# The first MLP's first tiles in four parts, pooled maxima scaled on ScalarE, and a new order of issue

## The chip, the cores and the metric

The kernel runs on one core of a Trainium2 chip. A core has five engines with an instruction stream each: TensorE (PE in the profile; its weight loads are listed as PEld), VectorE (DVE), ScalarE (ACT), GpSimd (POOL) and SyncE (SP), which here only issues DMAs. The engines wait for each other through semaphores, and each works through its own stream in the order in which the program was written. The metric is the device time of one launch in microseconds; the median of three runs is compared.

## What is computed

Two attentions over the same q, k and v are added, one over positions pooled in fours and one over a band of seven neighbours; the sum is the input of two MLPs in a row.

```python
q_d = q.reshape(B, H, Sd, 4, D).mean(axis=3)          # B=4, H=8, S=576, Sd=144, D=64
out_d = sm_attn(q_d, k_d, v_d)                        # softmax attention, pooled
out_up = np.repeat(out_d, 4, axis=2)
mask = np.abs(pos[:, None] - pos[None, :]) < 4        # the band
out_local = softmax(where(mask, q @ k.T / 8, -1e9)) @ v
x = (out_up + out_local).transpose(0, 2, 1, 3).reshape(2304, 512)
h = x @ moe_w_in                                      # 512 -> 2048
x = np.maximum(0.01 * h, h) @ moe_w_out               # 2048 -> 512
h = x @ moe2_w_in
out = where(h >= 1, h, where(h <= -1, 0, (h + 1) ** 2 / 4)) @ moe2_w_out
```

## The kernel before

**Tiling.** The 2304 tokens go through each MLP in five blocks of 512, 512, 512, 512 and 256. Every MLP operand is held as two f16 halves, high and low, and a product is three products of halves (high by high, high by low, low by high). In the first MLP `g1` (L1922) makes one tile of the hidden layer, 128 features by 512 tokens: twelve 128x512 matmuls (L1934), three for each of the four 128-row chunks `c` of the input, into one PSUM bank. A chunk `c` of the input is one pair of heads. ACT and DVE turn the tile into two halves (L2046, L2172, L2176), and `g2` (L2196) adds its share of the second product into four further banks. The second MLP makes each product by a seven-product scheme on half-size operands: `s1` to `s4` (products at L1964) with copies on ACT (L1995) and sums on DVE (L2003, L2006, L2013) between them, and then two passes over the second weight (`pass1`, `pass2`, products at L2133), whose results are drawn together on DVE (`onto`, L2154) and stored (L2165).

**Attention.** `prep` (L1128) loads q and k and transposes them on PE (L1185), with copies on ACT (L1209). `local_p` does the banded attention of the first 16 of 36 pieces as matmuls (scores L1497 to L1512, row maximum on DVE at L1525, exponent on ACT at L1530, transposes L1553, product with v L1570, result to f16 halves at L1594 and L1600); `local_d` does the others on DVE alone (L1705 to L1779). `down` does the pooled attention, one pair of heads at a time: sums of four on DVE (L1278, L1280, L1287), scores on PE (L1353), then, for each of the two heads, `peak` on DVE (L1367 takes the maximum, L1368 multiplies it by minus the scale), `pexp` on ACT (L1375, two exponents that take the result as bias), the reciprocal, `norm` (on DVE at L1392, or on ACT at L1388 for the batches in `NORM_ACT_D`), transposes (L1402) and the product (L1420).

**Weights.** They come as 64-bit numbers and are turned into f16 halves: three DVE operations on integers (L701, L707, L713), one on ACT (L727) and one on DVE (L729) for the first MLP, and a like chain (L852 to L877) for the second, which then also needs sums of quarters (L961, L1056, L1063).

**What sets the order.** The program is written by a planner, `Issue.run`: all operations are given a key (a due time in steps of the MLPs, shifted by tables such as `DUE`, `G2LATE`, `LAG7`, `PASS2`), an estimated duration and their dependences, and the planner plays the five engines forward in time. Whenever an engine is free in its estimate, it takes the ready operation with the lowest key. What results is a fixed order for each engine. Where PE has nothing ready in the plan before the time `FILL`, the planner writes in a product with zeros (L2529, 128x512, called a filler below), which keeps PE's clock up and whose result nobody reads. After `FILL` an idle PE in the plan leaves no trace in the program.

**PSUM.** There are eight banks, handed out by `Banks`; once the MLPs have begun, six of the eight are kept for them.

Of the kernel before, what the change touches and what calls it, by code (L numbers as in the profile page):

```python
# [15 lines left out]
AX = mybir.AxisListType.X  # L16
# [11 lines left out]
LEAD_O = 2  # L28
WINDOW_O = 15
OUT_GAP = 0.411  # L30
LAG7 = {0: 10, 1: 9, 2: 15, 3: 18, 4: 10}
# [4 lines left out]
T4_LATE = 12  # L36
EARLY_O = 4
W1_SPARE = 1957
LATE1 = 5.273
# [4 lines left out]
WINDOW_T = 7  # L44
# [5 lines left out]
WINDOW_A = 19  # L50
WINDOW_D = 15
LEAD_W = 6
LEAD_W1 = 1.5
LEAD_W1O = 1.477
RUSH_B = {1: 7.782}
RUSH_P = None
W1_RUSH = 0
QUEUE = 2.793
# [3 lines left out]
WINDOW_B = {2: 6, 3: 6}  # L62
# [5 lines left out]
DMA_END = 1.377  # L68
SW_END = 2.263
# [6 lines left out]
RUN_PE = 0.06  # L76
# [6 lines left out]
D_PE = 24.191  # L83
D_STRETCH = 1.006
W1_FROM = 9
W1_MORE = 1.467
# [10 lines left out]
PEAK_D = 4921  # L97
RESERVE = 3947
HP_GAP = 0.8
RESERVE_W = 0  # L100
SPARE = 5950

TWO_FROM = (2, 98)
WINDOW = 22
WINDOW_W = 34
LIMIT = 26744
AHEAD = 5
LEAD_Q = (12, 8)
O_LATE = 1.34
LAGMAX = 5  # L110
G2KEY = 1.87

NORM_ACT = (1,)
NORM_ACT_D = (1,)
FILL = 173.83


DUE = {0: -0.12, 2: 0.03, 3: -0.01, 9: 2.8, 10: -0.4, 14: -3.31, 17: -9.75, 19: -0.21,
# [129 lines left out]
class Issue:  # L248
# [4 lines left out]
    SHAPE = 0.093  # L253

# [36 lines left out]
    def run(self, fill=None):  # L291
# [16 lines left out]
        while left:  # L308
# [94 lines left out]
class Banks:  # L403
# [24 lines left out]
def kernel(  # L428
# [36 lines left out]
    QB = 64  # L465
# [48 lines left out]
    T_SC = 0.553  # L514
# [222 lines left out]
    class Pair:  # L737


        def __init__(self, n, nu):  # L740
# [3 lines left out]
            self.ready = []  # L744

# [1823 lines left out]
```

## Time and profile before

| | us |
|---|---|
| median of 3 runs (820.48 to 821.06) | 820.82 |
| the profiled execution | 821.11 |
| its span, first to last instruction | 819.3 |
| PE busy | 812.0 |
| DVE busy | 726.5 |
| ACT busy | 499.1 |

The profiled execution has 1.8 us outside its span. A PE matmul is listed with its whole way through the array, 379 ns for 128x512, while the next one begins 216 ns after it: neighbouring matmuls overlap, and the pace is read from starts, not from durations. For the same reason the profile calls PE busy while a filler runs. An idle time is printed with the engine and line that ended it.

### The profile page before, as it was taken

The numbers are of one execution on the slowest core, as the hardware profiler recorded it, in microseconds if no ns is written. First come the engines' busy times: TensorE is split into PE (matmuls) and PEld (weight loads), VectorE is DVE, ScalarE is ACT, GpSimd is POOL, SyncE is SP. The second block draws the span as 40 slices with busy tenths as digits, with TensorE's granted clock in tenths as the row PEclk, the third lists the DMA queues.
The fourth block names the chain that finished last, engine by engine and source line by source line (L and its number), as shares of the span: only waits on it lengthen the run. The fifth ranks groups of instructions, "written<-read, shape, count | busy, mean of one in ns | idle before, by whom it ended". The sixth has DMA issues, their size and how long they took to land. (4 is left out here: it accounts for less than half of the span.)

```text
span 819.3 us, 17419 instructions
## 1 busy us (share of the span) xinstructions
PE 812.0 (99%) x6791; PEld 562.6 (69%) x6791; DVE 726.5 (89%) x1360; ACT 499.1 (61%) x1283; POOL 38.7 (5%) x60
## 2 busy tenths in 40 slices
PE   9999999999999999999999999999999999999997
PEld 6765554544454444544446888888888888889986
DVE  4999999999999999999999999999669697896761
ACT  4987667466436463473356677777567676775640
POOL 1010000033001310000000000000000000000000
PEclk9999999999999999999999999999999999999999
DMA  8877556576345822331733320010000200100001
GB/s 207 207 193 232 190 187 172 155 145 126 92 124 168 134 44 69 100 103 55 253 103 129 110 73 27 2 52 27 26 2 14 78 14 2 52 27 2 3 27 52
DMA packets 63521, 77.40 MB, mean 94 GB/s; under 512 B 17742, under 2 KB 41678, under 8 KB 63438
## 3 DMA queue, kind: packets, MB, share of 16 engines
q1 hardware_dynamic: 52238, 72.13, 28.4%
q0 software_dynamic: 11200, 4.15, 4.5%
q8 instruction: 53, 0.87, 0.4%
q14 instruction: 30, 0.25, 0.1%
HBM read 66.80 MB, written 9.44 MB: 93 GB/s over the span
## 5 line engine op out<-in xcount | busy, mean ns | idle before, releaser
L1934 PE MATMUL bank<-arena,w 128*128 128x512 f16 (+1 forms) x960 | 197.0, 358 | 0.0
L2196 PE MATMUL bank<-arena,w 128*128 128x512 f16 x768 | 176.4, 379 | 0.3 <-DVE arena L2176 0.3
L1934 PEld LDWEIGHTS <-w 128*128 128x128 f16 x960 | 92.5, 98 | 88.9 <-issue 1.9
L2196 PEld LDWEIGHTS <-w 128*128 128x128 f16 x960 | 92.0, 98 | 86.9 <-issue 2.3
L2133 PEld LDWEIGHTS <-w 128*128 128x128 f16 x1086 | 106.0, 98 | 12.2
L2133 PE MATMUL bank<-arena,w 128*128 128x256 f16 x810 | 96.8, 273 | 0.0
L1964 PEld LDWEIGHTS <-w 128*128 128x128 f16 x960 | 86.4, 98 | 10.0 <-issue 1.3
L2046 ACT ACTIVATE arena<-bank 128x512 f32<-128x512 f32 x64 | 38.0, 593 | 81.5 <-PE bank L1934 79.2
L2050 ACT ACTIVATE w<-bank,half 128x512 f32<-128x512 f32 x66 | 45.3, 687 | 41.5 <-DVE bank L2013 38.8
L1964 PEld LDWEIGHTS <-arena 128*128 128x128 f16 x720 | 64.8, 98 | 6.7
L2099 ACT ACTIVATE w<-w 128x256 f16<-128x256 f32 (+1 forms) x112 | 50.2, 478 | 17.4 <-DVE w L2058 13.2
L1964 PE MATMUL bank<-arena,w 128*128 128x256 f16 (+1 forms) x480 | 59.9, 267 | 0.6 <-DVE bank L2006 0.4
L2058 DVE SCALAR_TENSOR_TENSOR w<-w,bank 128x512 f32<-128x512 f32 x66 | 44.8, 681 | 15.0 <-ACT w L2054 14.0
L2103 DVE SCALAR_TENSOR_TENSOR w<-w 128x256 f16<-128x256 f32 (+1 forms) x112 | 53.1, 502 | 3.6 <-ACT w L2099 3.5
L1964 PE MATMUL bank<-w,w 128*128 128x256 f16 (+1 forms) x480 | 52.6, 256 | 0.0
L1995 ACT COPY w<-bank 128x256 f32<-128x256 f32 x106 | 36.4, 365 | 18.2 <-PE bank L1964 16.5
L2133 PEld LDWEIGHTS <-arena 128*128 128x128 f16 x426 | 41.6, 98 | 5.5 <-issue 0.7
L1964 PE MATMUL bank<-arena 128*128 128x256 f16 (+1 forms) x384 | 44.6, 266 | 0.0
L2176 DVE SCALAR_TENSOR_TENSOR arena<-arena 128x512 f16<-128x512 f32 x64 | 43.6, 682 | 0.3 <-ACT arena L2172 0.3
L1779 DVE TENSOR_TENSOR arena<-arena 128x768 f32<-128x768 f32 (+2 forms) x60 | 41.1, 687 | 1.4
L2054 ACT ACTIVATE w<-w 128x512 f32<-128x512 f32 x66 | 41.1, 628 | 1.2
L2172 ACT ACTIVATE arena<-arena 128x512 f16<-128x512 f32 x64 | 40.3, 630 | 0.9
(219 smaller groups left out, 1342.0 us busy)
## 6 DMA issues: line engine op xcount, KB each, us to landing
arena<-in_moe_w_in_dram SPq DMA_DIRECT2D x15, 1024.0 KB
arena<-in_moe_w_out_dram SPq DMA_DIRECT2D x8, 1024.0 KB
arena<-in_moe_w_out_dram SPq DMA_DIRECT2D x9, 512.0 KB
arena<-x SPq DMA_DIRECT2D x4, 1024.0 KB
x<-arena SPq DMA_DIRECT2D x15, 256.0 KB
w<-in_moe_w_out_dram SPq DMA_DIRECT2D x7, 512.0 KB
out_dram<-w SPq DMA_DIRECT2D x14, 256.0 KB
arena<-in_k_dram SPq DMA_DIRECT2D x23, 112.0 KB
```

The costliest lines, as they stand in the source:

```text
L1779: nc.vector.tensor_tensor(out, x, y, op=ALU.add)
L1934: nc.tensor.matmul(h[:, e], a[:, f // FP, c, f % FP], y[:, :, c, :], start=(n == 0), stop=(n == 3 * KDM - 1),)
L1964: nc.tensor.matmul(o[:, e], a[:, i, c], y[:, k, c, :], start=first and e == 0 and n == 0, stop=n == 5, skip_group_check=True,)
L2050: nc.scalar.activation(out=t, in_=st["h", p], func=AF.Relu, scale=0.5 * s_in, bias=half)
L2054: nc.scalar.activation(out=t, in_=t, func=AF.Square, scale=s_in ** -0.5)
L2058: nc.vector.scalar_tensor_tensor(out=t, in0=t, scalar=1.0 / s_in, in1=st["h", p], op0=ALU.min, op1=ALU.max)
L2099: nc.scalar.activation(out=left(p, part, q0, q1)[:, 0], in_=src(), func=AF.Copy, scale=so)
L2103: nc.vector.scalar_tensor_tensor(out=d[:, 1], in0=src(), scalar=so, in1=d[:, 0], op0=ALU.mult, op1=ALU.subtract)
L2133: nc.tensor.matmul(o[:, k], a[:, i, at:at + P], y[:, j], start=opens and p == e == k == n == 0, stop=p == PH - 1 and e == E - 1 and n == 2 ...
L2172: nc.scalar.activation(out=gv(p)[0], in_=st["t", p].ap, func=AF.Copy, scale=so)
L2176: nc.vector.scalar_tensor_tensor(out=lo, in0=st["t", p].ap, scalar=so, in1=hi, op0=ALU.mult, op1=ALU.subtract)
L2196: nc.tensor.matmul(o, a, y[:, e, :], start=(first and n == 0 and c % E == 0), stop=(last and n == 2), skip_group_check=True,)
```

## The change

The first three tiles (`EARLY = 3`) of the first MLP's first block are no longer made by one operation of twelve matmuls that waits for the whole input block. Each is four operations of three matmuls, one for each pair of heads, chained to one another, and each waits only for that pair's own part of the input (`x.by[c]`) and the weights. The bank is taken with the first part and stays taken until ACT has read the tile.

In `down` the maximum is taken with its sign turned (one DVE instruction), and the multiplication by the scale moves to ACT, as a small instruction ahead of the two exponents. `NORM_ACT_D` takes in batch 2, so the four normalisations of that batch (one DVE instruction on 72x576 each) become 16 on ACT (72x144 each).

The planner's estimates are altered: a result that is used on the engine that made it is ready at once, where 0.14 to 0.25 us were allowed before, and some durations and DMA latencies have other values. All tables of keys are new, so nearly every instruction stands elsewhere. A line of them and the rest of the diff:

```diff
-G2LATE = {0: 7.366, 1: 6.364, 2: 4.968, 3: 5.548, 4: 9.226}
-PASS2 = {0: 47.587, 1: 3.15, 2: 56.047, 3: 70.737, 4: 41.965}
+G2LATE = {0: 7.696146, 1: 10.971802, 2: 1.675998, 3: 4.854888, 4: 14.291468}
+PASS2 = {0: 45.397812, 1: 23.065416, 2: 37.189274, 3: 77.327851, 4: 66.686012}
+EARLY = 3
+EARLY_ROOM = 0
-NORM_ACT_D = (1,)
-FILL = 173.83
+NORM_ACT_D = (1, 2)
+FILL = 170.7754
...
-                    u.ready = max(u.ready, d + self.HOP[op.eng]
-                                  + (self.HOP_PE if u.eng == "PE" else 0.0))
+                    hop = 0.0 if u.eng == op.eng and not op.lat else (
+                        self.HOP[op.eng] + (self.HOP_PE if u.eng == "PE" else 0.0))
+                    u.ready = max(u.ready, d + hop)
...
+    def hold(self):
+        self.mlp += 1
+        return self.get()
...
-            nc.vector.reduce_max(ml(0, par), psv(par), axis=AX)
-            nc.vector.tensor_scalar_mul(ml(0, par), ml(0, par), -s_e)
+            nc.vector.reduce_max(ml(0, par), psv(par), axis=AX, negate=True)
 
         def pexp(par):
             if not par:
                 st["p"] = buf(4 * G, from_t)
             p = st["p"].ap[:GH].rearrange("p (h a g) -> p h a g", h=2, a=2)
+            nc.scalar.mul(ml(0, par), ml(0, par), s_e)
...
         x1[blk].ready.append(o)
+        x1[blk].by[hp].append(o)
...
-        def g1(p, i):
-            sch.step = max(sch.step, i)
-            h_open[0] += 1
+        def g1(p, i, cs=range(KDM)):
+            if KDM - 1 in cs:
+                sch.step = max(sch.step, i)
+                banks.begun = True
...
-            st["h", p] = banks.get(True)
+            if 0 in cs:
+                h_open[0] += 1
+                st["h", p] = banks.hold()
...
-                n = 0
-                for c in range(KDM):
+                n = 3 * cs[0]
+                for c in cs:
...
-            o1 = sch.add(
+            o1 = None
+            if m == 1 and not b and p < EARLY:
+                for c in range(KDM):
+                    o1 = sch.add(
+                        "PE", 3 * t_mm(N) * E, lambda p=p, i=i, c=c: g1(p, i, (c,)),
+                        x.by[c] + [o1] + [w_ready[m, 0, f] for f in fs], key=float(i),
+                        banks=0 if c else 1, mlp=True, cols=3 * 512,
+                        gate=None if c else (lambda: len(banks.free) > EARLY_ROOM))
+            o1 = o1 or sch.add(
```

How it moves the instructions, at three places. The first is PE's stream where the first MLP begins; L2529 and L2554 are the fillers, L1934 and L1951 the products of `g1`, in the kernel before and in the changed one. Before:

```order
L1185 MATMUL bank_64<-ident,arena 64x64 x8
L2529 LDWEIGHTS zeros
L2529 MATMUL bank_63<-zeros 128x512
...
L1353 MATMUL bank_67<-w_61 72x144
L1353 MATMUL bank_69<-w_61 72x144
...
L1934 LDWEIGHTS w_79
L1934 MATMUL bank_68<-arena,w_79 128x512
...
L1934 MATMUL bank_65<-arena,w_79 128x512
...
L2529 LDWEIGHTS zeros
L2529 MATMUL bank_70<-zeros 128x512
```

And after:

```order
L1523 MATMUL bank_66<-arena 64x70 x8
L1951 LDWEIGHTS w_79
L1951 MATMUL bank_69<-arena,w_79 128x512
...
L1581 MATMUL bank_65<-arena 64x64 x8
L1581 MATMUL bank_70<-w_61,arena 64x64 x8
...
L1564 MATMUL bank_70<-ident,w_61 70x128 x4
L1951 LDWEIGHTS w_79
L1951 MATMUL bank_69<-arena,w_79 128x512
...
L2554 LDWEIGHTS zeros
L2554 MATMUL bank_63<-zeros 128x512
```

Before, two whole tiles (banks 68 and 65) stand in a row once the attention of the block is through, after three fillers; after, the first tile (bank 69) stands in threes between the products of the last pairs of heads. The stream as a whole has 51 fillers before and 41 after, and the same number of each other product.

The second place is where the pooled maxima stand on DVE, first before and then after:

```order
L1367 TENSOR_REDUCE w_61<-bank_69 72x2
L1368 TENSOR_SCALAR w_61<-w_61 72x2
L1278 TENSOR_TENSOR arena<-arena 72x4x128
L1280 TENSOR_TENSOR w_61<-arena 72x2x2x64
L1367 TENSOR_REDUCE w_61<-bank_64 72x2
```

```order
L1378 TENSOR_REDUCE w_61<-bank_70 72x2
L1536 TENSOR_REDUCE w_61<-bank_65 128x4
L1378 TENSOR_REDUCE w_61<-bank_64 72x2
L1298 TENSOR_REDUCE w_61<-w_61 128x144
L1289 TENSOR_TENSOR arena<-arena 72x4x128
```

and on ACT after, where L1384 is the new multiplication and L1386 the exponents:

```order
L1384 ACTIVATE w_61<-w_61 72x2
L1386 ACTIVATE w_61<-bank_70,w_61 72x144 x2
L1220 ACTIVATE w_61<-bank_66 128x64x5
L1541 ACTIVATE w_61<-bank_65,w_61 128x70 x4
L1568 COPY w_61<-bank_67 70x512
L1220 ACTIVATE w_61<-bank_68 128x64x4
L1384 ACTIVATE w_61<-w_61 72x2
```

DVE has one instruction less for each of the 32 maxima, and ACT one more, which stands directly ahead of the exponents that need it; eight of the 32 stand in the attention of the first batch.

The third place is the end of PE's stream, where the last two blocks' second passes stand; the rows are those at which the bank changes. Before:

```order
L2133 MATMUL bank_64<-arena,w_79 128x256
...
L2133 MATMUL bank_63<-arena,w_79 128x256
...
L2133 MATMUL bank_67<-arena,w_79 128x256
...
L2133 MATMUL bank_64<-arena 128x256
...
L2133 MATMUL bank_70<-arena,w_79 128x256
```

And after:

```order
L2150 MATMUL bank_63<-w_79 128x256
...
L2150 MATMUL bank_69<-arena 128x256
...
L2150 MATMUL bank_64<-arena,w_79 128x256
...
L2150 MATMUL bank_63<-arena,w_79 128x256
...
L2150 MATMUL bank_64<-arena,w_79 128x256
```

Before, the last bank (70) belongs to a 512-token block, and DVE's last instruction reads 128x512 of it for a store of 256 KB. After, the long stretch of the 512-token block (bank 69) stands further forward, between the passes of the 256-token block, whose last read is 128x256 for a store of 128 KB.

## Rows read from the trace of the kernel before

**Rows 1.** The page: span, busy time and instructions of each engine

```profile
span 819.3 us, 17419 instructions
...
PE 812.0 (99%) x6791; PEld 562.6 (69%) x6791; DVE 726.5 (89%) x1360; ACT 499.1 (61%) x1283; POOL 38.7 (5%) x60
```

**Rows 2.** Busy us by stretch (A:B length, PE, PEld, DVE, ACT, POOL, clock, DMA, GB/s)

```profile
0.00:40.00 40.00, 38.80 (x637) 27.11 (x639) 28.02 (x89) 28.05 (x125) 5.39 (x24) 1.00 0.80 208
40.00:80.00 40.00, 40.00 (x511) 24.99 (x506) 38.60 (x101) 32.34 (x117) 4.04 (x8) 1.00 0.76 211
...
520.00:560.00 40.00, 39.64 (x363) 35.24 (x361) 39.08 (x85) 30.23 (x64) 0.00 (x0) 1.00 0.10 34
560.00:600.00 40.00, 40.00 (x369) 35.86 (x367) 31.76 (x68) 24.61 (x54) 0.00 (x0) 1.00 0.06 21
```

**Rows 3.** What PE waited for: us in total, times, longest us

```profile
PE bank L2529 <- DVE half L533: 1.2, 1, 1.2
PE bank L2133 <- DVE w L2154: 0.5, 1, 0.5
PE bank L1964 <- DVE bank L2006: 0.4, 1, 0.4
PE bank L2196 <- DVE arena L2176: 0.3, 1, 0.3
PE bank L1964 <- DVE bank L2013: 0.2, 1, 0.2
```

**Rows 4.** PE's timeline near 115 us: start us, us, line, operation

```profile
113.56 1.04 PE L2529 MATMUL bank<-zeros 128*128 128x512 bf16 x4
114.52 0.57 PE L1570 MATMUL bank<-w,arena 70*64 70x64 f32 x12
...
115.25 2.75 PE L1934 MATMUL bank<-arena,w 128*128 128x512 f16 x12
```

**Rows 5.** DVE's timeline there: the low half of a weight

```profile
113.40 1.22 DVE L729 SCALAR_TENSOR_TENSOR w<-w,w 128x1024 f16<-128x1024 f32 x1
```

**Rows 6.** DVE's timeline near 18 us

```profile
17.85 0.45 DVE L1367 TENSOR_REDUCE w<-bank 72x2 f32<-72x288 f32 x1
18.33 0.17 DVE L1368 TENSOR_SCALAR w<-w 72x2 f32<-72x2 f32 x1
18.41 0.68 DVE L1278 TENSOR_TENSOR arena<-arena 72x512 f32<-72x512 f32 x1
...
20.58 0.45 DVE L1525 TENSOR_REDUCE w<-bank 128x4 f32<-128x280 f32 x1
20.95 0.74 DVE L1287 TENSOR_REDUCE w<-arena 128x144 f32<-128x576 f32 x1
```

**Rows 7.** By source line: duration ns min/median/max, first and last start

```profile
L1367 DVE TENSOR_REDUCE w<-bank x16: 443/446/454, 17.9 to 136.6; 72x2 f32<-72x288 f32 x16
...
L1392 DVE TENSOR_TENSOR arena<-arena x8: 746/748/748, 195.9 to 331.4; 72x576 f32<-72x576 f32 x8
```

**Rows 8.** ACT by line and shape, first 60 us: its smallest work

```profile
L1375 ACT ACTIVATION_READ_ACCUMULATOR w<-bank,w 72x1 f32 x6 | 1.2, 208 | 0.0
...
L1594 ACT ACTIVATE arena<-w 128x64 f16<-128x64 f32 x4 | 1.0, 258 | 0.0
```

**Rows 9.** The end: DVE's last reads

```profile
806.88 0.42 DVE L2154 SCALAR_TENSOR_TENSOR w<-bank,w 128x256 f32<-128x256 f32 x1 [3.58 <-PE bank L2133]
...
814.67 0.69 DVE L2154 SCALAR_TENSOR_TENSOR w<-bank,w 128x512 f32<-128x512 f32 x1 [4.55 <-PE bank L2133]
```

**Rows 10.** The end, busy us by stretch: a store of 128 KB, one of 256 KB

```profile
808.10:808.70 0.60, 0.60 (x8) 0.53 (x7) 0.00 (x0) 0.00 (x0) 0.00 (x0) 1.00 0.63 219
...
816.20:817.20 1.00, 0.00 (x0) 0.00 (x0) 0.00 (x0) 0.00 (x0) 0.00 (x0) 1.00 0.74 262
```

**Rows 11.** SP's timeline: the first load of q for batch 1

```profile
25.93 0.36 SPq L1140 DMA_DIRECT2D arena<-in_q_dram  x1
```

**Rows 12.** PE's timeline: the first use of it

```profile
38.13 1.26 PE L1185 MATMUL bank<-ident,arena 64*64 64x64 f32 x36
```

More of the change, by code (lines that the diff above doesn't have):

```diff
@@ L27 @@
 OUT7 = (0,1,2,3,4)
-LEAD_O = 2
+LEAD_O = 5
 WINDOW_O = 15
-OUT_GAP = 0.411
-LAG7 = {0: 10, 1: 9, 2: 15, 3: 18, 4: 10}
-G2LATE = {0: 7.366, 1: 6.364, 2: 4.968, 3: 5.548, 4: 9.226}
-PASS2 = {0: 47.587, 1: 3.15, 2: 56.047, 3: 70.737, 4: 41.965}
+OUT_GAP = 0.357325
+LAG7 = {0: 9, 1: 10, 2: 18, 3: 18, 4: 12}
+G2LATE = {0: 7.696146, 1: 10.971802, 2: 1.675998, 3: 4.854888, 4: 14.291468}
+PASS2 = {0: 45.397812, 1: 23.065416, 2: 37.189274, 3: 77.327851, 4: 66.686012}
 SOON = 1000.0
 FP = 2
-T4_LATE = 12
+EARLY = 3
+EARLY_ROOM = 0
+T4_LATE = 10.083883
 EARLY_O = 4
-W1_SPARE = 1957
-LATE1 = 5.273
+W1_SPARE = 4178
+LATE1 = 8.896926
 LEAD_S = 4
@@ L43 @@
 LEAD_T = 4
-WINDOW_T = 7
+WINDOW_T = 9
 LEAD = 5
@@ L49 @@
 RUSH = 1.0e4
-WINDOW_A = 19
-WINDOW_D = 15
+WINDOW_A = 17
+WINDOW_D = 13
 LEAD_W = 6
-LEAD_W1 = 1.5
-LEAD_W1O = 1.477
-RUSH_B = {1: 7.782}
+LEAD_W1 = 1.06903
+LEAD_W1O = 1.731533
+RUSH_B = {1: 6.558924}
 RUSH_P = None
 W1_RUSH = 0
-QUEUE = 2.793
+QUEUE = 2.681077
 WHOLE = ()
@@ L61 @@
 POOLED = ()
-WINDOW_B = {2: 6, 3: 6}
+WINDOW_B = {2: 8, 3: 6}
 LEAD_D = 2
@@ L67 @@
 DMA_LAST = 0.85
-DMA_END = 1.377
-SW_END = 2.263
+DMA_END = 1.710062
+SW_END = 1.886638
 SW_FIRST = 1.88
@@ L75 @@
 RUNS = (0, 1)
-RUN_PE = 0.06
+RUN_PE = 0.061
 RUN_ACT = 1.1
@@ L82 @@
 LAT_W = (1.95, 1.95)
[L83 to L86, printed above, removed]
+D_PE = 80
+D_STRETCH = 0.856281
+W1_FROM = 6
+W1_MORE = 1.972363
 D_ACT = (0,1)
@@ L96 @@
 ADD_PE = ()
-PEAK_D = 4921
-RESERVE = 3947
-HP_GAP = 0.8
+PEAK_D = 5103
+RESERVE = 218
+HP_GAP = 0.756178
 RESERVE_W = 0
-SPARE = 5950
+SPARE = 5409
 TWO_FROM = (2, 98)
-WINDOW = 22
-WINDOW_W = 34
-LIMIT = 26744
+WINDOW = 27
+WINDOW_W = 24
+LIMIT = 26572
 AHEAD = 5
-LEAD_Q = (12, 8)
-O_LATE = 1.34
+LEAD_Q = (10, 5)
+O_LATE = 4.600221
 LAGMAX = 5
-G2KEY = 1.87
+G2KEY = 0.5
 NORM_ACT = (1,)
-NORM_ACT_D = (1,)
-FILL = 173.83
-DUE = {0: -0.12, 2: 0.03, 3: -0.01, 9: 2.8, 10: -0.4, 14: -3.31, 17: -9.75, 19: -0.21,
[7 rows of a table removed]
+NORM_ACT_D = (1, 2)
+FILL = 170.7754
+DUE = {0: -0.01, 2: -0.09, 3: -10.68, 4: 1.18, 5: -0.17, 7: -0.38, 9: 8.62, 10: -0.31,
[9 rows of a table added]
 class Arena:
@@ L253 @@
     SHAPE = 0.093
+    SAME = True
     FREE = 0.14
@@ L744, in __init__ @@
             self.ready = []
+            self.by = {c: [] for c in range(KDM)}
         def make(self):
@@ L1225, in prep @@
                 n = (NA, QBB - NA)[i]
-                t = ch.op("PE", pe_mm(RUN_PE * 2 * n, QB, 2 * n, D) if b in RUNS else pe_tr(QB, n, QB), lambda nm=nm, i=i: tr(nm, i), [ld[nm]], banks=1, shape=(1, 1) if b in RUNS else (2, 2),
+                t = ch.op("PE", pe_mm(0.05 + RUN_PE * 2 * n, QB, 2 * n, D) if b in RUNS else pe_tr(QB, n, QB), lambda nm=nm, i=i: tr(nm, i), [ld[nm]], banks=1, shape=(1, 1) if b in RUNS else (2, 2),
                           after=(lambda nm=nm: st[nm].free(),) if i else ())
@@ L1447, in down @@
         for par in range(2):
-            e = ch.op("DVE", 0.56, lambda par=par: peak(par), [o, e], need=() if par else (8,))
-            x = ch.op("ACT", 2 * t_act(G, True, 2), lambda par=par: pexp(par), [e, x],
+            e = ch.op("DVE", t_dve(2 * G), lambda par=par: peak(par), [o, e], need=() if par else (8,))
+            x = ch.op("ACT", 2 * t_act(G, True, 2) + 0.1, lambda par=par: pexp(par), [e, x],
                       need=() if par else (4 * G,),
@@ L1861, in local_d @@
                 reds.append(o)
-            o = ch.op("DVE", 0.36 + 0.16 * sum((r == 0) + (r + n == SEGB) for _, n, _, r in rr),
+            o = ch.op("DVE", 0.36 + 0.32 * sum((r == 0) + (r + n == SEGB) for _, n, _, r in rr),
                       lambda par=par: soft1(par), reds, need=(L,))
@@ L1898, in local_d @@
                 ch.op("DVE", t_dve(512), lambda jh=jh: xl(jh), [h], after=freer(("x", jh))))
+            for by in x1[blk].by.values():
+                by.append(ch.ops[-1])
         ch.close()
```

2 lines of the change are left out of this document (1 added, 1 removed), and 16 rows, old and new, of the table DUE.

## The prediction

> **What bounds the kernel now.** I read the page first, then busy time by stretches of 40 us, then what PE waited for, then single places in the timelines. The page says that PE is busy for 812.0 of 819.3 us [rows 1]. That could mean that only PE's own work counts. But the stretches show that DVE is as full as PE for two thirds of the span: 38.6 of 40 us between 40 and 80 us, 39.1 between 520 and 560 us (the stretches between are like these two), and only from 560 us on does it fall to 31.8 [rows 2]. And each wait of PE that the profile prints, after the start, ended with a DVE instruction: 0.5, 0.4, 0.3 and 0.2 us, together 1.4 us [rows 3]. So PE and DVE run level up to about 560 us, and PE alone sets the pace behind that. The granted clock is 1.00 in every stretch, 2.4 GHz, and is not in play. The first 40 us are another regime: DVE and ACT are busy for 28 us each and wait for loads and for each other [rows 2], and PE fills its holes with products of zeros.
>
> Of those there are 51 before and 41 after. They are real time on PE, and the other products are the same in number, so the change can gain on PE in two ways only: fewer fillers and fewer waits.
>
> **The change part by part.**
>
> *Fillers.* Four in a row take from 113.56 to 114.52 us, 0.24 us each [rows 4]. Ten fewer: 10 x 0.24 = 2.4 us less on PE. At the pace of 216 ns of two 512-column products in a row it is 2.2 us; I take 2.4.
>
> *Whether DVE can follow.* The fillers at 113.56 cover a wait: the weight half that DVE makes from 113.40 to 114.62 us [rows 5] is of the kind that the product at 115.25 [rows 4] multiplies with, and between its end and the product lie 0.6 us. So of a group of fillers the last half microsecond or so is more than the wait needed, and the rest stood for DVE. If PE is to run 2.4 us earlier from here on, DVE must deliver some 1.8 us earlier. It gets this from two edits. A maximum with its scaling takes from 17.85 to 18.41 us, 0.56 us; a reduction of nearly the same size that is not followed by a user of its result takes from 20.58 to 20.95, 0.37 us [rows 6]. The sign in the instruction and the scaling on ACT thus save 0.19 us for each of 32 maxima. Sixteen of them stand before 137 us [rows 7], 16 x 0.19 = 3.0 us; the others are in the later batches, 3.0 us more. The four normalisations of batch 2 that leave DVE have 0.75 us each, about 0.67 in a stream where neighbours overlap, 2.7 us in all, after 190 us [rows 7]. So DVE has 3.0 us by 137 us, more than the 1.8 that it needs, and 8.7 us by 331 us. I charge nothing here; the price of a failure is the 2.4 us (first rival).
>
> *Waits of PE.* With DVE that far ahead, the 0.3 us at L2196, in the middle of the kernel, should go. The 0.5 us at L2133 is at the very end, where PE waits for DVE to have read the bank that it writes next; in the new order 48 products of another block stand between, so it goes. The 0.4 and 0.2 us at L1964 [rows 3] come from the chain copy, sum, product inside the second MLP, and I leave two thirds of them. Sum: -1.0 us, of at most -1.4 and at least 0.
>
> *The end.* DVE's last read becomes one of 256 columns instead of 512: 0.42 instead of 0.69 us [rows 9]. The last store becomes one of 128 KB: such a one moved within 0.6 us, one of 256 KB needed 1.0 us [rows 10]. Nothing else runs there, so both count in full: -0.27 - 0.4 = -0.7 us.
>
> *ScalarE.* It gets 32 small multiplications and 16 normalisations. No row shows a multiplication of 72x2. The nearest are the read of an accumulator, 0.21 us for one column, and a scaling of 64 columns, 0.26 us [rows 8]. After 40 us ACT has idle time to hide them, 7.7 us in the stretch from 40 to 80 [rows 2], and no wait of PE was ended by ACT [rows 3], so these 40 cost nothing; uncovered, the 24 multiplications among them alone would be 24 x 0.21 = 5.0 us. But eight multiplications stand in the attention of the first batch, at the start, where each of the three engines waits for the others. From below their cost is zero, since the chain of one pair of heads is no longer than before: 0.17 us of scaling on DVE [rows 6] goes, about 0.21 on ACT comes. From above it is 8 x 0.26 = 2.1 us, if ACT's stream is what the start waits for. ACT is busy for 28.0 of the first 40 us [rows 2], and part of the 12 idle ones lies before the first data; I take 0.8 us, a little under half of 8 x 0.21.
> The Trainium skill ("ScalarE: Activation LUTs", section "Rules for kernel authors") speaks against this edit: it tells one to put a multiplication on VectorE, not ScalarE. The same page (section "What ACT_TABLE_LOAD costs") gives 186 ns for an operation with constants as scale and bias, plus 0.83 ns an element, so an estimate by it is 0.19 us each, 1.5 us for the eight with nothing hidden. No run here shows the operation yet.
>
> *The product in four parts.* The products stay twelve to a tile, so PE's work is as before; the parts of the first tile fill holes between other products in the attention of the last pairs of heads. That is where fillers went, so the gain is in the first term. The wait that is new is that of a part for its pair of heads: PE works in order, and all of its stream is queued behind. The bank that the tile holds for longer is one of eight. I take zero.
>
> *The second MLP's order.* The number of products between a copy's source and the user of the sum falls from 18 to 12 at four places by the new order. The wait that such a place showed was 0.4 us [rows 3]; four of them would be 1.6, none 0. I take one, +0.4 us.
>
> **Sum:** -2.4 - 1.0 - 0.7 + 0.8 + 0.4 = -2.9 us. The profiled execution has 821.11 us, of which 819.3 are its span, so 818.2 for it. The median lies 0.29 below it at 820.82; from there, **817.9 us**.
>
> **The rivals.**
>
> *First, no change: the fillers come back as waits.* PE has 10 fillers fewer, but DVE, ACT and the loads deliver when they did, and what DVE saves is lost in waits of its own. For it: DVE and PE are level, so any hole of DVE is at once one of PE. Against it: the DVE work that goes is more than is needed. The 2.4 us return: 820.3 us.
>
> *Second, no change: ACT becomes the bound of the start.* The eight multiplications cost 2.1 us instead of 0.8, and the start moves by 1.3 us: 819.2 us. For it: the three engines wait for each other there; against it: ACT is 30% idle.
> This is what the rule of the Trainium skill ("ScalarE: Activation LUTs", "Rules for kernel authors") amounts to here.
>
> *Third, faster still.* All 1.4 us of waits go, ACT hides all and the second MLP's new order costs nothing: -2.4 - 1.4 - 0.7 = -4.5, 816.3 us.
>
> *Fourth, slower: loads at the start.* The new order of SP's DMAs puts weights further forward. Up to and with batch 1's first load of q, 6.70 MB are asked for instead of 5.65; at 208 GB/s [rows 2] the 1.05 MB are 5.0 us. Before, that load is issued at 25.93 us [rows 11] and its data are used at 38.13 [rows 12], 12.2 us later; 5.0 us later and used about 1.3 us earlier, by the products that stand ahead of it, 5.9 us are left. That is enough for 0.3 MB at this rate. If the queues are deeper than that, PE waits there with all of its stream behind it. A delay of 5 us more than that slack would give 817.9 + 5 = 822.9 us; it turns the sign from 2.9 us on. For it: the DMA engines are 80% busy at the start [rows 2]. Against it: SP itself waits for buffers more than the data wait for a queue.
>
> That the change does not do what it says is excluded by the order: 41 fillers, 36 instructions fewer on DVE and 48 more on ACT are there.
>
> **How the numbers follow.** A measurement of this kernel can tell about 0.2% (1.6 us) from no change, that is, times under 819.2 or over 822.5 us. My forecast has 0.47, the first rival 0.20, the second 0.10, the third 0.10, the fourth 0.13. Faster: 0.47 + 0.10 = 0.57; same: 0.20 + 0.10 = 0.30; slower 0.13. The range goes from the third case, 816.3, to 821.2: that takes in both cases of no change with some of the upper ends of the unknown costs (0.9 us above 820.3), and leaves out the fourth.
>
> **What would show it.** Right: PE's busy time down by about 2.4 us, with no new wait of PE over 0.5 us before 60 us; the instruction at the new maximum taking 0.37 us to the next; the wait at the last passes gone; DVE's last read 0.42 us long. The first rival would show as PE waits between 40 and 200 us that add up to about 2 us, ended by DVE or ACT. The second as an ACT that is busy 30 us or more of the first 40 and ends PE's waits. The fourth as a wait of PE at the transposes (L1185 before) ended by a DMA. The forecast is wrong if PE's waits as a whole exceed those of before.

## The result, and the profile after

The change makes the kernel slower. After: 825.79 us, median of 6 runs (823.96 to 828.19). Before, on the same chip: 820.69 us, median of 6 (820.45 to 822.38). The ratio is 1.0061 with a 95% interval of 1.0043 to 1.0078, so +5.1 us. The forecast was 817.9, 7.9 us too low, and the result lies outside its range of 816.3 to 821.2. The profiled execution of after has 825.57 us, of which 823.8 are its span.

The page of after, span and busy time, against [rows 1]:

```profile
span 823.8 us, 17396 instructions
...
PE 812.9 (99%) x6781; PEld 562.1 (68%) x6781; DVE 726.1 (88%) x1324; ACT 515.8 (63%) x1331; POOL 38.8 (5%) x60
```

DVE has 36 instructions fewer, and yet its busy time went down by 0.4 us only, from 726.5 to 726.1. Keep that row in mind: it holds most of the answer. PE's busy time, which was to fall by about 2.4 us, rose by 0.9.

Busy time by stretches of 40 us, the kernel after (columns as in [rows 2]):

```profile
0.00:40.00 40.00, 38.49 (x605) 26.77 (x607) 27.52 (x79) 26.96 (x118) 4.02 (x22) 1.00 0.98 227
40.00:80.00 40.00, 39.84 (x515) 24.61 (x512) 39.11 (x96) 31.01 (x106) 3.30 (x9) 1.00 0.74 197
...
360.00:400.00 40.00, 38.91 (x186) 18.06 (x184) 38.97 (x55) 19.86 (x51) 0.00 (x0) 1.00 0.29 96
...
440.00:480.00 40.00, 38.59 (x337) 32.80 (x336) 39.62 (x54) 24.94 (x41) 0.00 (x0) 1.00 0.46 159
480.00:520.00 40.00, 39.03 (x357) 34.67 (x356) 39.12 (x77) 32.26 (x65) 0.00 (x0) 1.00 0.04 15
520.00:560.00 40.00, 40.00 (x368) 35.72 (x366) 34.70 (x76) 30.27 (x65) 0.00 (x0) 1.00 0.10 34
```

The same stretches before, where they did not stand in [rows 2]:

```profile
360.00:400.00 40.00, 39.91 (x190) 18.46 (x188) 39.56 (x56) 15.46 (x26) 0.00 (x0) 1.00 0.35 122
...
440.00:480.00 40.00, 39.79 (x352) 34.26 (x351) 39.86 (x53) 25.98 (x44) 0.00 (x0) 1.00 0.37 133
480.00:520.00 40.00, 39.99 (x367) 35.67 (x366) 39.79 (x84) 33.44 (x70) 0.00 (x0) 1.00 0.04 15
```

The start is nearly as it was. The loss lies in the middle: in the nine stretches from 160 to 520 us PE is idle for 5.3 us, before for 0.6, and DVE is full there in both kernels. The clock is 1.00 in all of these stretches. Lined up in the two traces by the share of its columns that PE has done (fillers left out, f32 columns counted four times), PE is 1.4 us ahead of before at 32% (202 us) and 5.5 us behind at 68% (519 us). So a part of the gain was there at first and was lost later.

What PE waited for in the kernel after, against [rows 3]:

```profile
PE bank L2213 <- DVE arena L2193: 1.9, 4, 1.1
PE bank L2554 <- DVE half L543: 1.2, 1, 1.2
PE bank L1981 <- ACT w L2012: 1.1, 1, 1.1
PE bank L1981 <- DVE bank L2023: 1.0, 2, 0.7
PE bank L1951 <- ACT arena L1386: 0.5, 1, 0.5
PE bank L1981 <- DVE w L2075: 0.2, 1, 0.2
PE bank L1951 <- DVE arena L1755: 0.2, 1, 0.2
PE bank L1413 <- ACT w L1541: 0.2, 1, 0.2
```

Without the start (L2554) that is 5.1 us where the forecast had 0.4 of 1.4 left. None of these waits was ended by a load. DVE ends 3.3 us of them: it is late, although it was given less work. ScalarE ends 1.8 us, where before it ended none.

The end is what was forecast. DVE's last reads, against [rows 9]:

```profile
817.54 0.42 DVE L2171 SCALAR_TENSOR_TENSOR w<-bank,w 128x256 f32<-128x256 f32 x1 [4.55 <-PE bank L2150]
820.24 0.43 DVE L2171 SCALAR_TENSOR_TENSOR w<-bank,w 128x256 f32<-128x256 f32 x1 [2.27 <-PE bank L2150]
```

From the start of the last read to the end of the span it was 819.3 - 814.67 = 4.6 us and is now 823.8 - 820.24 = 3.6 us.

**The theory, and its rivals.** Two stretches of DVE's timeline suggest a cause. Around 466 us in the kernel after:

```profile
461.64 2.15 DVE L1074 TENSOR_TENSOR arena<-arena 128x512 f32<-128x512 f32 x3
463.70 0.68 DVE L1067 TENSOR_TENSOR w<-arena,w 128x512 f16<-128x512 f32 x1
...
466.65 0.68 DVE L863 TENSOR_SCALAR w<-arena 128x1024 int32<-128x1024 int32 x1
467.37 1.23 DVE L869 SCALAR_TENSOR_TENSOR w<-arena,w 128x1024 int32<-128x1024 int32 x1
468.51 0.68 DVE L2193 SCALAR_TENSOR_TENSOR w<-w 128x512 f16<-128x512 f32 x1
```

And the same kinds of work before:

```profile
463.05 0.68 DVE L852 TENSOR_SCALAR w<-arena 128x1024 int32<-128x1024 int32 x1
463.65 0.68 DVE L1063 TENSOR_TENSOR arena<-arena 128x512 f32<-128x512 f32 x1
464.26 1.21 DVE L858 SCALAR_TENSOR_TENSOR w<-arena,w 128x1024 int32<-128x1024 int32 x1
```

Before, another instruction stands between the first step of a weight's conversion (L852) and the second (L858), which reads what the first has written; it starts 0.60 us after the first. After, the second step (L869) stands right behind the first (L863), and it starts 0.72 us later, when the first has ended (466.65 + 0.68 = 467.33). Of the three differences at L1074, two have a reader of their result right behind them; from the first to the instruction behind the third it takes 2.06 us instead of 3 x 0.60 = 1.80, 0.13 for each of the two. So, by these rows, **an instruction that reads what the one just ahead of it on DVE has written costs DVE 0.12 us more.** The new rule of the planner, by which a reader on the same engine counts as ready at once, packs such instructions back to back. I counted in the two programs how many DVE instructions wait for the one just ahead of them, among DVE's first 800 (up to 490 us before, 510 after): 168 before, and without the 32 scalings that went to ScalarE 137 of these; 216 after. That is 80 more, 9.6 us at 0.12. The traces bear the count out roughly: among the first 800, the neighbours of which the second starts 0 to 0.1 us behind the first one's end are 177 before, 147 in the run with only the scalings moved (before_scale_act below), and 217 after, which is 70 more.

Theory A is this. Its rivals: B, the product in parts and the missing fillers; C, the multiplications on ScalarE; D, the loads at the start; and A2, that the order does put later work ahead of what PE needs next, but that the waits cost nothing.

### The profile page after: what moved, and what is told of

The parts are those of the page before. It is cut to its first block, busy times and chain, and to the rows that moved or that the text cites. A ratio compares the mean times of both kernels' runs of the same rounds, so it can differ in the third digit from the quotient of the medians.

```text
span 823.8 us, 17396 instructions
## 1 busy us (share of the span) xinstructions
PE 812.9 (99%) x6781; PEld 562.1 (68%) x6781; DVE 726.1 (88%) x1324; ACT 515.8 (63%) x1331; POOL 38.8 (5%) x60
## 4 chain that ended last, share of the span: by engine, by line
PE 53%; DVE 37%; issue 4%; ACT 4%; DMA 1%; SPq 1%; DVEq 0%; ACTq 0%
PE bank L2150 17%; PE bank L1981 14%; PE bank L1951 6%; PE bank L2213 6%; DVE arena L1791 4%; DVE arena L1717 3%; DVE arena L2193 3%; DVE arena L1725 3%; DVE arena L1761 2%; PE bank L1196 2%; DVE arena L888 2%; DVE arena L869 2%; DVE arena L972 2%; DVE w L888 2%; DVE arena L875 1%
## 5 line engine op out<-in xcount | busy, mean ns | idle before, releaser
L1951 PE MATMUL bank<-arena,w 128*128 128x512 f16 (+1 forms) x960 | 195.6, 358 | 0.7 <-ACT arena L1386 0.5
L2213 PE MATMUL bank<-arena,w 128*128 128x512 f16 (+1 forms) x792 | 178.0, 376 | 2.1 <-DVE arena L2193 1.9
L2213 PEld LDWEIGHTS <-w 128*128 128x128 f16 x960 | 92.4, 98 | 89.9 <-issue 5.3
L1951 PEld LDWEIGHTS <-w 128*128 128x128 f16 x960 | 92.2, 98 | 89.2 <-issue 2.9
L1981 PEld LDWEIGHTS <-w 128*128 128x128 f16 x960 | 86.4, 98 | 11.7 <-issue 2.5
L2150 PEld LDWEIGHTS <-w 128*128 128x128 f16 x876 | 85.5, 98 | 9.8
L2150 PE MATMUL bank<-arena,w 128*128 128x256 f16 x624 | 76.3, 273 | 0.0
L1981 PEld LDWEIGHTS <-arena 128*128 128x128 f16 x720 | 64.9, 98 | 8.3 <-issue 1.7
L2150 PEld LDWEIGHTS <-arena 128*128 128x128 f16 x636 | 62.0, 98 | 7.1
L1981 PE MATMUL bank<-w,w 128*128 128x256 f16 (+1 forms) x528 | 58.5, 258 | 0.1
L2150 PE MATMUL bank<-arena 128*128 128x256 f16 x456 | 55.8, 273 | 0.0
L2116 ACT ACTIVATE w<-w 128x256 f16<-128x256 f32 (+1 forms) x101 | 44.3, 462 | 18.3 <-DVE w L2075 13.4
L1981 PE MATMUL bank<-arena,w 128*128 128x256 f16 (+1 forms) x432 | 53.8, 266 | 1.3 <-DVE bank L2023 1.0
L2120 DVE SCALAR_TENSOR_TENSOR w<-w 128x256 f16<-128x256 f32 (+1 forms) x101 | 46.8, 486 | 0.4 <-ACT w L2116 0.2
L1981 PE MATMUL bank<-w,arena 128*128 128x256 f16 (+1 forms) x384 | 44.0, 259 | 0.2 <-DVE w L2075 0.2
```

The lines of the kernel that those rows point to most:

```text
L1951: nc.tensor.matmul(h[:, e], a[:, f // FP, c, f % FP], y[:, :, c, :], start=(n == 0), stop=(n == 3 * KDM - 1),)
L1981: nc.tensor.matmul(o[:, e], a[:, i, c], y[:, k, c, :], start=first and e == 0 and n == 0, stop=n == 5, skip_group_check=True,)
L2116: nc.scalar.activation(out=left(p, part, q0, q1)[:, 0], in_=src(), func=AF.Copy, scale=so)
L2120: nc.vector.scalar_tensor_tensor(out=d[:, 1], in0=src(), scalar=so, in1=d[:, 0], op0=ALU.mult, op1=ALU.subtract)
L2150: nc.tensor.matmul(o[:, k], a[:, i, at:at + P], y[:, j], start=opens and p == e == k == n == 0, stop=p == PH - 1 and e == E - 1 and n == 2 ...
L2213: nc.tensor.matmul(o, a, y[:, e, :], start=(first and n == 0 and c % E == 0), stop=(last and n == 2), skip_group_check=True,)
```

## Experiments

All ratios are against the kernel before, run on the same chip beside each kernel. Times of different kernels come in part from different chips, so a difference of two medians and the one by the ratios can be some tenths of a microsecond apart.

| kernel | us | ratio (95%) |
|---|---|---|
| after | 825.8 | 1.0061 (1.0043 to 1.0078) |
| after_scale_dve | 829.8 | 1.0102 (1.0087 to 1.0117) |
| after_whole | 830.2 | 1.0105 (1.0083 to 1.0128) |
| before_scale_act | 820.9 | 0.9998 (0.9990 to 1.0007) |
| after_spread | 833.3 | 1.0146 (1.0133 to 1.0159) |
| after_spread_weights | 830.7 | 1.0121 (1.0107 to 1.0134) |
| after_nodep | 821.1 | 1.0000 (0.9991 to 1.0009) |
| after_nodep_norm | 819.6 | 0.9980 (0.9970 to 0.9990) |
| after_hop_dve | 822.3 | 1.0019 (1.0010 to 1.0027) |
| before_newhop | 844.9 | 1.0287 (1.0273 to 1.0301) |
| before_scale_nofill | 819.0 | 0.9972 (0.9961 to 0.9983) |
| before_tail | 820.9 | 1.0000 (0.9991 to 1.0009) |
| before_combo | 817.6 | 0.9954 (0.9942 to 0.9967) |
| before_combo26 | 815.5 | 0.9934 (0.9920 to 0.9947) |

### The edits one by one, the order left as it is

The planner's costs were not touched, only what is issued at a place.

after_scale_dve:

```diff
-            nc.vector.reduce_max(ml(0, par), psv(par), axis=AX, negate=True)
+            nc.vector.reduce_max(ml(0, par), psv(par), axis=AX)
+            nc.vector.tensor_scalar_mul(ml(0, par), ml(0, par), -s_e)
...
-            nc.scalar.mul(ml(0, par), ml(0, par), s_e)
```

> The kernel after in its own order, with only the scaling of the 32 maxima back on VectorE. Theory A: VectorE, already late, gets 32 x 0.19 = 6.1 us more: 829 to 832 us. Rival C (ScalarE has become the bound): 820 to 823, since ScalarE loses 32 x 0.2 = 6.4 us. Rivals B and D: 825.8 within 1.

829.8 us: 4.0 slower than after by the medians, 3.4 by the ratios, as theory A has it. The multiplications on ScalarE are not what makes the new order slow. (The change also moved batch 2's normalisations to ScalarE; that was not run by itself.)

after_whole:

```diff
                 st["h", p] = banks.hold()
+            if KDM - 1 not in cs:
+                return
+            cs = range(KDM)
```

> The kernel after in its own order, with only the parts undone: the first three tiles' products are issued whole, at the place of their last part. Rival B (parts hold a bank and make PE wait for their pair of heads): 821 to 824. Theory A: the parts' work (9 parts of 6 products, 9 x 0.65 = 5.9 us at most) loses its place in PE's holes at the start, so 825.8 to 830, not faster.

830.2 us in the median, but the six runs fall apart. Three with a granted clock of 0.993 or 0.994 took 831.4 to 832.5 us, three with 1.000 took 826.4, 826.9 and 829.1. So without the loss of clock the kernel is about 1 us slower than after, and the rest of the 4.4 us is clock; the last section shows it in the trace. Rival B falls as far as the parts go: undoing them is not faster. (A part is three products, not six as the expectation has it; 0.65 us is the time of three.) The bank is still taken at the first part's place, so what holding it longer costs was not tested, and neither were the ten missing fillers in this order.

before_scale_act is the edit of after_scale_dve the other way round, in the kernel before.

> The kernel before in its own order, with only the maxima negated by the reduction and scaled on ScalarE. Theory A: the edit itself is harmless; VectorE is 6.1 us further ahead and PE's 1.4 us of waits can shrink: 818.5 to 820.7. Rival C: slower than before by 2 us or more, 822.8 and up.

820.9 us, no change. So ScalarE carries the multiplications without loss; but DVE, with 723.3 us of busy time instead of 726.5, brings nothing either. In this order, work taken from DVE alone does not pay; before_scale_nofill below gives PE something to start earlier.

### Two attempts to move the dependent instructions apart

In after_spread the order's DVE instructions are kept, but one that directly follows its source lets the next, independent one go first; the instructions of all other engines keep their order.

```diff
-                    best.fn()
+                    self.emit(best)
...
+        if self.held is None and not op.need and self.last in op.deps:
+            self.held = op
+            return
```

> The kernel after, with one thing changed: where a VectorE instruction would directly follow the VectorE instruction whose result it reads, it is issued one VectorE instruction later, behind an independent one (PE, ScalarE, the DMAs and the planner's numbers stay as they are; 49 such pairs fewer among the first 800 VectorE instructions, 58 in all). Theory A (the new order puts dependent VectorE instructions back to back, 0.12 us each): VectorE gains 49 x 0.12 = 5.9 us by about 500 us, so 820 to 822 us instead of 825.8, and PE's waits for VectorE between 200 and 520 us go down by 4 to 6 us. Rival B (the product in parts and the missing fillers), rival C (the multiplications on ScalarE), rival D (loads at the start): no change, 825 to 826.5.

833.3 us: 7.5 slower, against theory A as it stood. PE's waits before products of the attention grew by 4.3 us, from 0.2 in after, and one in the second MLP from 1.1 to 3.1. The longest of each kind:

```profile
PE bank L2007 <- ACT w L2038: 3.1, 1, 3.1
...
PE bank L1439 <- ACT arena L2215: 1.5, 1, 1.5
```

The operands of these products of the attention come over a chain through DVE and ScalarE. My reading is that the normalisation in such a chain, put behind an independent instruction, came late where that one had itself to wait for ScalarE; no row here shows it. So I left these chains alone and moved only the weights' conversions and sums (after_spread_weights: the same with a mark on those chains, and up to two held back).

> The kernel after; only in the conversion of weights and the sums over weight blocks, a VectorE instruction that would directly follow the one whose result it reads is issued one or two places later, the attention's chains keep their places (36 such pairs fewer, 31 of them among the first 800 VectorE instructions). The first such run moved the attention's chains too, and PE waited longer for these. Theory A: 31 x 0.12 = 3.7 us: 821.5 to 823.5. Theory A2: 825 to 827.

830.7 us: 4.9 slower. The largest wait of PE in it, and what ScalarE did then (line, start, duration, idle before):

```profile
PE bank L2023 <- ACT w L2054: 3.1, 1, 3.1
```

```profile
470.14 0.63 ACT L2231 ACTIVATE w<-w 128x512 f16<-128x512 f32 x1
474.37 1.06 ACT L925 ACTIVATE w<-w 128x1024 f16<-128x1024 f32 x1 [3.60 <-DVE w L915]
475.34 1.18 ACT L2054 COPY w<-bank 128x256 f32<-128x256 f32 x4
```

ScalarE works in order. It stands for 3.6 us before L925, a weight's high half, which needs the third step of its conversion (L915), the very instruction that was moved back. Behind it waits the copy L2054 for PE's next product. In the kernel after the same wait stands at the same place, with 2.36 us on ScalarE and the 1.1 us at L1981 above; so the move added 1.2 us on ScalarE and 2.0 on PE. PE's hole then cost some of its clock as well (the column before the last two):

```profile
472.00:476.00 4.00, 0.86 (x8) 0.59 (x6) 3.48 (x5) 1.63 (x4) 0.00 (x0) 0.91 0.79 250
476.00:480.00 4.00, 4.00 (x26) 3.01 (x25) 3.86 (x6) 2.25 (x5) 0.00 (x0) 0.66 0.62 245
```

Both runs failed as tests of the price of 0.12 us: they neither show it nor speak against it. They show that one place later on DVE can cost far more than that on the engines behind it.

### The waits taken away, every instruction in its place

after_nodep leaves number, size and order of all instructions as they are, and lets the instructions of the weights' conversion and sums work on other words than those that the one just ahead wrote.

```diff
-                out=f32(), in0=words()[1], scalar=-0x40000000, in1=f32(),
+                out=words()[0], in0=words()[1], scalar=-0x40000000, in1=words()[1],
...
-            steps = (("11", "12", "11"), ("12", "22", "12"), ("22", "22", "11"),
-                     ("21", "21", "22"))
+            steps = (("11", "11", "11"), ("12", "12", "12"), ("22", "22", "22"),
+                     ("21", "21", "21"))
```

> The kernel after, every instruction in its own place, but in the conversion of the weights and in the sums over weight blocks VectorE reads and writes other words than those of the instruction just ahead (so the weights' values are not the reference's; the number, size and order of all instructions are). 43 VectorE instructions fewer among the first 800 wait for the one just ahead of them. Theory A (each such wait costs VectorE 0.12 us): 43 x 0.12 = 5.2 us less by about 500 us: 820.5 to 822.5 instead of 825.8. Theory A2 (VectorE's lateness comes from the order's placing of later work ahead of what PE needs next, not from the waits): 825 to 826.5.

821.1 us: 4.7 of the 7.9 us are gone (5.0 by the ratios), 0.11 to 0.12 for each of the 43 waits. DVE's timeline at the place shown above, and two stretches of the kernel:

```profile
462.55 0.69 DVE L863 TENSOR_SCALAR w<-arena 128x1024 int32<-128x1024 int32 x1
463.15 1.22 DVE L869 SCALAR_TENSOR_TENSOR arena<-arena 128x1024 int32<-128x1024 int32 x1
464.29 0.69 DVE L2193 SCALAR_TENSOR_TENSOR w<-w 128x512 f16<-128x512 f32 x1
```

```profile
360.00:400.00 40.00, 39.61 (x188) 18.43 (x187) 39.29 (x53) 20.41 (x52) 0.00 (x0) 1.00 0.24 88
...
440.00:480.00 40.00, 40.00 (x357) 34.69 (x356) 39.30 (x55) 26.64 (x44) 0.00 (x0) 1.00 0.44 156
```

The second step now starts 0.60 us after the first, behind the same neighbour, and PE's holes at 360 to 400 and 440 to 480 us shrink from 1.09 and 1.41 us to 0.39 and 0. Theory A2 falls in the form in which the waits cost nothing. That the order places later work ahead as well is not excluded by it, and the traces show some of that: when PE has done 64% of its columns, at 475.2 us before and 480.0 after, DVE has behind it 422.8 us of work before and 426.3 after (each instruction at the shortest length of its shape, the scalings left out), though after no longer has the normalisations of batch 2. The busy time of DVE goes from 726.1 to 722.5 us with the same 1324 instructions.

Open was the rest of 3.2 us. after_nodep_norm takes 19 more of these waits away: the normalisations multiply by the maxima instead of by the reciprocals made just ahead of them.

```diff
+                l = st["ml"].ap[:GH, 0:4]
                 nc.vector.tensor_tensor(
                     p, p, l.unsqueeze(2).to_broadcast([GH, 4, G]), op=ALU.mult
                 )
...
+                sm = st["ml"].ap[:, :cnt]
```

> As after_nodep, and the normalisations on VectorE multiply by the maxima instead of by the reciprocals that the instruction just ahead has made (values are not the reference's; number, size and order of all instructions stay). 62 instead of 43 VectorE instructions fewer among the first 800 wait for the one just ahead. Theory A: 19 x 0.11 = 2.1 us less than after_nodep (821.1): 818.5 to 819.7. If the 3.2 us that after_nodep still lies above the forecast come from elsewhere (loads, ScalarE): 820.6 to 821.6.

819.6 us. By the ratios 0.2% or 1.6 us of the 2.1 expected; the medians differ by 1.5. So 62 waits less make 6.2 us, 0.10 each. With the 18 that are left at the same price the kernel would come to 817.8. That is worked out, not run. In the nine stretches from 160 to 520 us PE is now idle for 1.9 us (2.5 in after_nodep, 5.3 in after, 0.6 before); what the rest of it comes from is open.

### The planner's rule by itself

Here the planner makes another order, so more than the rule differs; but the end that the planner reckons for its own order tells how far the chip falls behind it. For before that is 820.7 - 812.5 = 8.2 us, for after 825.8 - 810.9 = 14.9.

```diff
-                    hop = 0.0 if u.eng == op.eng and not op.lat else (
+                    hop = 0.05 * (u.eng == "DVE") if u.eng == op.eng and not op.lat else (
```

> The kernel after with one number of its planner changed: a VectorE instruction counts as ready 0.05 us after the VectorE instruction that it reads from, not at once (ScalarE and PE keep the new rule). The planner then makes another order of its own, with 72 VectorE instructions fewer among the first 800 that wait for the one just ahead (144 instead of 216; 168 in the kernel before) and with 57 fillers; by its own reckoning this order ends 3.5 us later (814.4 against 810.9). Theory A: the chip falls behind the plan by as much as in the kernel before, some 8 us, not by the 14 of the kernel after: 821 to 824, faster than after. If the waits don't matter, the chip adds 14 to the plan: 827 to 830, slower than after.

822.3 us, 7.9 behind its plan. The order that looks 3.5 us worse to the planner is 3.5 us better on the chip. The other direction, before_newhop, puts the new rule, word for word as in the change, into the kernel before.

> The kernel before with one rule of its planner changed as in the change: on the same engine a reader counts as ready at once. The planner makes another order: 250 instead of 168 VectorE instructions among the first 800 wait for the one just ahead, 91 fillers instead of 51, and by its own reckoning an end at 823.5 instead of 812.5 us. Theory A: the chip adds 8 us as in the kernel before and 82 x 0.12 = 9.8 us for the waits: 837 to 842. If the waits don't matter: 831 to 833.

844.9 us, 21.4 behind its plan: 13.2 more than before, where 9.8 were expected. The sign is clear; the size is not explained by the count alone.

### The terms of the sum, in the order of before

before_scale_nofill is before_scale_act without the last ten fillers:

```diff
-        for ps in to:
+        made[0] += bool(to)
+        for ps in to[:made[0] <= 41]:
```

> The kernel before in its own order with the maxima scaled on ScalarE and without the last ten fillers (those after 70 us). By the prediction's first term: 10 x 0.24 = 2.4 us faster than the run with the scaling alone (820.9): 818.5. By its first rival: PE waits instead, 820 to 821. With theory A VectorE is 3.0 us ahead by then, so at least half of it should show: 818.5 to 819.8.

819.0 us; by the ratios 0.0026 x 821 = 2.1 us less than with the scaling alone. In this order, with DVE ahead, the fillers are worth what the prediction said. Whether DVE has to be ahead for it was not run.

before_tail takes only the due times of the last passes (`PASS2`) from after.

> The kernel before with only the due times of the last passes of the second MLP taken from the kernel after (products of two blocks alternate at the very end; nothing moves ahead of that). By the prediction's terms for the end (0.7) and for the wait at the last passes (0.5): 819.5 to 820.2, against 820.8 of before.

820.9 us, no change. But these numbers alone do not make the new end in the order of before: the last read is still one of 512 columns, and PE's wait of 0.5 us for it stands. It was not the test that it was meant to be. before_combo moves one number of the same table, and adds before_scale_nofill.

```diff
-PASS2 = {0: 47.587, 1: 3.15, 2: 56.047, 3: 70.737, 4: 41.965}
+PASS2 = {0: 47.587, 1: 3.15, 2: 56.047, 3: 70.737, 4: 70.0}
```

> The kernel before in its own order with the maxima scaled on ScalarE, without the last ten fillers, and with one due time of the last passes changed (block 4's from 42.0 to 70), so that the last read is one of 256 columns behind products of another block, as in the kernel after. By the prediction's terms the end gives 0.7 and the wait there 0.5: 819.0 - 1.2 = 817.8. If the end is worth nothing: 819.

817.6 us; by the ratios 1.5 us less than before_scale_nofill (1.2 expected). Its last read:

```profile
811.51 0.42 DVE L2154 SCALAR_TENSOR_TENSOR w<-bank,w 128x256 f32<-128x256 f32 x1 [2.25 <-PE bank L2133]
```

before_combo26 leaves out 15 more fillers (26 in place of 41 in the code above).

> As before_combo, but only the first 26 of the 51 fillers are left (none after 32.3 us; 15 fewer again, 3.6 us of PE). If fillers are real time as long as VectorE can follow (it is 3 us ahead by 137 us): 814.5 to 816. If between 32 and 70 us they only stand in waits for the loads and the attention: as before_combo, 817.3 to 818.3.

815.5 us, on the slow side of the first expectation: of 3.6 us about 1.6 show, by the ratios, whose intervals still touch those of before_combo. The rest became waits, the largest of them one in the attention:

```profile
PE bank L1353 <- DVE w L1287: 1.3, 1, 1.3
```

This kernel is 0.66% faster than before, and so the fastest of all: the edit on ScalarE, fewer fillers and the shorter end, in the old order. Its granted clock is 1.00 from 0 to 40 and from 40 to 80 us, so the clock did not need the 25 fillers.

## Why the prediction was wrong

*The step that failed is "Whether DVE can follow", where I charged nothing.* I counted what the edits take from DVE (8.7 us) and let the rest of its stream run as fast as before. The new order makes that stream slower: 70 to 80 more instructions right behind their source, 0.10 to 0.12 us each, 7.0 to 9.6 us. Of the 7.9 us between forecast and result, 4.7 go with 43 of these waits and 6.2 with 62; the last 1.7 are not shown. The waits by themselves about use up the gain of 8.7. That after is slower than before takes more, and the work placed ahead is a second term that I had not looked for. At 64% of PE's columns an estimate from the traces is -6.1 for the 32 scalings, +3.5 for that work (the normalisations that went are in it already) and +7.0 to +9.6 for the waits, together 4.4 to 7.0 us, and PE is 4.7 us later there. The 3.5 us have no experiment of their own. The price was in my rows: in [rows 6] the scaling at L1368 starts 0.48 us after the maximum that it reads, while a reduction without a reader behind it takes 0.37. I booked the 0.19 us as a saving of the edit; 0.11 of it was the price of standing right behind one's source, and I did not ask how many such places the new order makes. The changed rule of the planner was in the diff to read.

*Fillers, -2.4:* right in size in the order of before with the scalings moved (2.1 us; PE's busy time 808.9 us, 811.9 with the fillers), not realised in the new order, where PE's busy time rose from 812.0 to 812.9. Busy time does not fall with the fillers when PE gets small waits instead: a 512-column product is listed with 379 ns while its successor can start after 216, so a wait shorter than the difference stays within busy time.

*Waits, -1.0:* wrong sign. From 1.4 to 5.1 us. The prediction named this as the sign of its being wrong.

*The end, -0.7:* right in kind, 1.0 us in the trace. With the wait that goes there, 1.5 us in before_combo.

*ScalarE, +0.8:* not needed, as far as the multiplications go. One takes what I estimated:

```profile
L1384 ACT ACTIVATE w<-w 72x2 f32<-72x2 f32 x16 | 3.2, 200 | 1.2 <-DVE w L1378 1.2
```

The scaling alone changed nothing in the order of before (820.9). ACT is busy for 26.96 us of the first 40 in the new order, under the 30 that the second rival asked for. That rival thus falls, and with it the rule of the Trainium skill ("ScalarE: Activation LUTs", section "Rules for kernel authors") for this place: DVE is the fuller engine here, and putting the work back on it cost 3.4 to 4.0 us in the new order. But the 40 pieces of work after 40 us were put at nothing because no wait of PE had been ended by ACT, and in the new order ACT ends 1.8 us; which part of that its new work has was not tested.

*The new maximum:* 0.37 us to the next, as forecast. Two of them in the kernel after:

```profile
24.94 0.82 DVE L1378 TENSOR_REDUCE w<-bank 72x2 f32<-72x288 f32 x2
25.68 0.15 DVE L584 TENSOR_SCALAR w<-w 128x4 f32<-128x4 f32 x1
```

*The second MLP's order, +0.4:* DVE's sums ended 1.0 us of waits at L1981 instead of 0.6, the 0.4 that was expected, but by luck: in after_nodep, whose order is the same, it is 0.6 again, so the fewer products between did not bring it by themselves.

```profile
PE bank L1981 <- DVE bank L2023: 0.6, 1, 0.6
```

The 1.1 us ended by ScalarE there come from the weight's conversion ahead of the copy.

*The fourth rival* had the sign right for another reason: none of the waits of PE listed for the kernel after was ended by a load. *The first* had the fillers return as waits. Its own sign, about 2 us of waits between 40 and 200 us, did not come: PE is idle for 0.4 us there. The waits came behind 200 us, and it did not foresee that DVE itself would slow down.

## What to carry to other kernels

Before you cost a new order, count for each engine that is full how many instructions stand right behind the one they read from, before and after; with the price taken from one row this is a term of the sum like any other. A planner that lets such a reader start at once fills a full engine with small gaps that it does not see, and the distance between its own end and the chip's shows it. And do not mend this by moving single instructions back: an engine that works in order behind them may lose more than the gap.

## What the runs showed of the hardware

A reader right behind its source on DVE starts 0.04 us after the source's record ends (466.65 + 0.68 = 467.33, start at 467.37). Without that dependence the next one starts 0.09 us before the record ends (462.55 + 0.69 = 463.24, start at 463.15). From start to start the step is 0.72 instead of 0.60 us, 0.12 more. This agrees with the Trainium skill ("Perfetto Trace Analysis", section "Per-instruction lifecycle: what the profiler-reported window actually captures"): the next instruction may begin to fetch its data once the engine has finished executing, while a semaphore is only pushed when the writes are acknowledged. Another page of the Trainium skill ("VectorE: DVE Perf Modes", section "The DRAIN you can't avoid") reports that eight copies with a semaphore after each take as long as with one after the last, so that the semaphore costs nothing extra there. It does not say whether its copies read one another; for a reader right behind its source the measured 0.10 to 0.12 us decide here.

In after_whole PE loses its parts, and with them what it did between 50 and 53 us. In the kernel after, two of the parts stand there:

```profile
50.95 0.82 PE L1951 MATMUL bank<-arena,w 128*128 128x512 f16 x3
...
52.05 0.81 PE L1951 MATMUL bank<-arena,w 128*128 128x512 f16 x3
```

```profile
48.00:52.00 4.00, 4.00 (x61) 2.73 (x59) 3.93 (x14) 2.52 (x14) 0.19 (x4) 1.00 0.75 188
52.00:56.00 4.00, 4.00 (x73) 2.80 (x71) 3.73 (x19) 2.66 (x11) 0.23 (x1) 1.00 0.87 264
```

The same stretches in after_whole, in its run of 832.1 us, and those behind them:

```profile
48.00:52.00 4.00, 2.75 (x26) 1.46 (x25) 3.90 (x15) 2.60 (x15) 0.19 (x4) 1.00 0.85 210
52.00:56.00 4.00, 3.52 (x60) 3.02 (x62) 3.76 (x17) 2.44 (x10) 0.11 (x1) 0.69 0.67 222
56.00:60.00 4.00, 4.00 (x40) 2.29 (x36) 2.06 (x8) 1.57 (x5) 1.08 (x1) 0.50 0.52 83
60.00:62.00 2.00, 2.00 (x21) 1.21 (x20) 1.75 (x5) 0.95 (x3) 0.00 (x0) 0.50 1.01 241
62.00:64.00 2.00, 2.00 (x6) 0.73 (x7) 1.97 (x4) 0.57 (x1) 0.00 (x0) 0.57 0.24 94
64.00:66.00 2.00, 2.00 (x11) 0.88 (x9) 0.34 (x1) 0.40 (x1) 0.00 (x0) 1.00 0.00 0
```

After a hole in which PE is busy for 2.75 of 4 us the granted clock falls to 0.50, that is 1.2 GHz, and it is back at 1.00 from 64 us on. Three of the six runs lost clock like this, and these are the longer ones: 831.4 to 832.5 us against 826.4 to 829.1 for the three at 1.000. So of the 4.4 us that the parts seem to be worth in the new order, all but about 1 us is that they keep PE at work, and with it the clock at 2.4 GHz, in the attention's thin places. Why the other three runs kept the clock is not shown; they have no trace. The same fall stands behind the hole in after_spread_weights above, where PE is busy for 0.86 of 4 us and the clock goes to 0.91 and 0.66 in two stretches.
